# A new order for the instructions of an attention and gated-MLP kernel

## The chip, the cores and the metric

The kernel runs on one core of a Trainium2 chip. The metric is the device time of one execution in microseconds (us), the median of several runs. A profile, taken in an execution of its own, gives the start and length of every instruction on the engines: TensorE (PE, its weight loads PEld), VectorE (DVE), ScalarE (ACT), GpSimd (POOL) and the DMA queue of SyncE (SP).

## The reference

For 8 batches and 12 heads of 448 rows by 64, q and k are normalised row by row and scaled by g_q and g_k; softmax attention gives x of 448 by 768 for each batch. Then a gated MLP follows:

```
rmsnorm(x, g) = x / sqrt(mean(x*x) + 1e-6) * g
attn = softmax(rmsnorm(q) @ rmsnorm(k).T / sqrt(64)) @ v        # heads side by side: x [8, 448, 768]
h = relu(x @ w_in);  u, v = h[..., :512], h[..., 512:]
v_n = (v - mean(v)) / sqrt(var(v) + 1e-6)                       # over the 512
v_s = w_spatial @ v_n + b_spatial                               # over the 448 rows
out = (u * v_s) @ w_out                                         # [8, 448, 768], float32
```

## The kernel before

Four heads of one batch make a group; there are 24 groups, G = 0 to 23, three for each batch b. All instructions stand in one hand-scheduled program. A table of words, PLAN, is read from front to back; each word calls one small function that issues one step, and so the table alone sets the order in which each engine gets its instructions and the DMA queue its loads. A word reads name.arguments/slots/engine; the engine is a (ACT), v (DVE) or g (POOL). With i = 0 for q, 1 for k and 2 for v, the words of the attention are:

- L.G.i loads a group's q, k or v into one of ten raw tiles; l, q, r, i, j, n, p, k are the same steps in halves for group 0.
- Q squares a raw tile into sqt, R sums the squares on DVE, I and J (ACT) make 1/rms from the sums of q and k, N multiplies raw by it into nrm (bf16).
- P transposes nrm on PE and K copies it out of PSUM into qT or kT; later groups use T, a transposing DMA, and Z, which scales k.
- S.G.u makes two blocks of scores on PE (8 matmuls of 32 columns wide weights), E.G.u is their exp on ACT into et (168 of each).
- F.G casts v into vt. The words s, a and b sum et against ones and against the two halves of vt, for groups G and G+1 at once; D and d (ACT) make 1/sum; X (DVE) multiplies it in and gives x, transposed, in xt.

The words of the MLP: V (v half) and U (u half) multiply by w_in, W does the last 64 rows of V with the last 64 of the output of the batch before, c and u are the relu evictions, B, M, m, A the normalisation, H the spatial product, G the gate, O the product with w_out, o its eviction, t the store. wi.h.l loads an eighth of w_in from POOL's queue, ws, wo and wb the other weights; wx and y put w_spatial and b_spatial in place. The first V word of a batch needs X of one group of that batch and all of w_in; the third needs all three groups.

z.n and h.n are idle words on PE: n matmuls of the identity, 448 and 64 columns wide, whose results nobody reads.

PSUM has eight banks, and a word's slot digits name the banks or buffers that it takes; it waits until the last reader of what stood there is done. Between POOL and DVE there is one more rule, in port(): the squares, N, F and some others wait for the latest instruction of that kind that the table put on the other of the two engines, so these two take turns in the table's order.

## Time and profile before

| | |
|---|---|
| median of 3 runs | 268.88 us (268.8 to 270.5) |
| the profiled execution, its own time | 271.01 us |
| its span, first to last instruction | 268.9 us |
| mean granted TensorE clock | 0.998 |
| PE busy | 250.4 us (93%) |
| ACT busy | 220.6 us (82%) |
| DVE busy | 210.6 us (78%) |
| POOL busy | 127.8 us (48%) |
| moved by DMA | 55.48 MB, 206 GB/s over the span |

The span is what the profile's times add up to; the execution's own time has 2.1 us more around it. Busy shares are means over the whole span, so the table says only which engine is fullest, not what is waited for in any one stage. A row of the timeline has start, length, engine, line, operation, output and inputs, how many instructions are merged in it, and in brackets how long the engine was idle before and for whom.

### The profile page before, as it was taken

Reading aid. Unit: us, or ns where it says so; the run is one execution under the profiler, and the core shown is the slowest. Engines: PE = TensorE matmul, PEld = TensorE weight load, DVE = VectorE, ACT = ScalarE, POOL = GpSimd, SP = SyncE. Lnnn points to the kernel's source line nnn. Section 1 sums busy time; section 2 is a strip of 40 time slices with the busy share of each in tenths; the row PEclk is TensorE's granted clock in tenths of the full one; section 3 lists DMA queues with packets and bytes.
Section 4 is the critical chain, followed back from the end, with each engine's and each line's share of the span. In section 5 each row is a group of like instructions: output and inputs, shape, how many; then the busy total and the mean of one; then the engine's idle time right before and its main releaser. Section 6 shows DMA issues by size and latency. Waiting matters only on the chain.

```text
span 268.9 us, 10005 instructions
## 1 busy us (share of the span) xinstructions
PE 250.4 (93%) x4311; PEld 127.8 (48%) x4311; DVE 210.6 (78%) x363; ACT 220.6 (82%) x363; POOL 127.8 (48%) x99
## 2 busy tenths in 40 slices
PE   5997775999999997999999999999999999999993
...
GB/s 250 369 257 335 236 255 140 313 227 307 195 218 269 268 249 305 289 247 256 213 261 207 162 252 272 307 221 151 125 166 126 63 58 148 71 51 0 88 115 210
DMA packets 58462, 55.48 MB, mean 206 GB/s; under 512 B 34609, under 2 KB 54130, under 8 KB 58418
## 3 DMA queue, kind: packets, MB, share of 16 engines
...
q8 instruction: 33, 0.54, 0.8%
...
HBM read 38.55 MB, written 11.01 MB: 184 GB/s over the span
## 4 chain that ended last, share of the span: by engine, by line
PE 79%; DMA 9%; issue 4%; POOL 3%; ACT 2%; DVE 1%; POOLq 0%; DVEq 0%
PE ps L544 17%; PE ps L655 14%; PE ps L683 12%; PE ps L509 11%; PE ps L589 11%; PE ps L669 9%; DMA raw<-in_k_dram 8%; PE ps L618 4%; DMA raw<-in_q_dram 1%; POOL sqt L385 1%; POOL nrm L437 1%; ACT et L517 1%; ACT sqt L383 1%; POOL nrm L429 1%; DVE ss L396 0%
## 5 line engine op out<-in xcount | busy, mean ns | idle before, releaser
L517 ACT ACTIVATE et<-ps 128x896 bf16<-128x896 f32 x168 | 146.4, 926 | 12.7 <-PE ps L509 10.7
L429 POOL TENSOR_TENSOR nrm<-raw,rs 128x896 bf16<-128x896 f32 x37 | 62.0, 1688 | 41.9 <-ACT rs L414 34.3
L509 PE MATMUL ps<-qT,kT 64*32 64x448 bf16 x1344 | 56.0, 353 | 4.1 <-ACT et L517 2.3
L396 DVE TENSOR_REDUCE ss<-sqt 128x14 f32<-128x896 f32 x46 | 48.5, 1074 | 2.2 <-POOL sqt L385 2.2
L385 POOL TENSOR_TENSOR sqt<-raw 128x896 f32<-128x896 f32 x24 | 40.1, 1677 | 11.7 <-DVE nrm L429 4.3
L544 PE MATMUL ps<-et,vt 64*32 64x448 bf16 x1344 | 41.9, 349 | 3.6 <-issue 2.3
L655 PE MATMUL ps<-xt,w_in 128*128 128x448 bf16 x192 | 43.2, 353 | 0.0
L573 DVE TENSOR_TENSOR xt<-ps,rc 128x448 bf16<-128x448 f32 x48 | 27.9, 619 | 14.6 <-PE ps L544 8.8
L589 PE MATMUL ps<-w_in,xt 128*128 128x512 bf16 x144 | 37.8, 380 | 0.0
L683 PE MATMUL ps<-w_out,gt 128*128 128x384 bf16 x192 | 36.2, 327 | 0.4 <-ACT et L517 0.4
L509 PEld LDWEIGHTS <-kT 64*32 64x32 bf16 x1344 | 20.1, 90 | 28.2 <-issue 19.5
L544 PEld LDWEIGHTS <-vt 64*32 64x32 bf16 x1344 | 21.9, 92 | 15.1 <-issue 5.8
L669 PE MATMUL ps<-w_spT,vn 128*128 128x448 bf16 (+1 forms) x128 | 27.3, 353 | 0.0
L655 PEld LDWEIGHTS <-w_in 128*128 128x128 bf16 x192 | 17.6, 98 | 20.1 <-issue 4.8
L366 DVE COPY os<-ps 128x384 f32<-128x384 f32 (+1 forms) x32 | 17.6, 555 | 12.0 <-PE ps L683 7.9
L683 PEld LDWEIGHTS <-gt 128*128 128x128 bf16 x192 | 17.7, 98 | 16.5 <-issue 4.3
L674 DVE TENSOR_TENSOR gt<-ps,us 128x448 bf16<-128x448 f32 x32 | 19.0, 620 | 7.6 <-PE ps L669 5.5
L544 PE MATMUL ps<-et,ones 64*32 64x448 bf16 x672 | 23.5, 350 | 0.6 <-ACT et L517 0.6
L320 POOL CAST vt<-raw 128x896 bf16<-128x896 f32 x16 | 14.8, 930 | 18.1 <-DVE us L582 7.9
L630 DVE BATCH_NORM_STATS2 s<-vs 128x6 f32<-128x512 bf16 (+1 forms) x32 | 21.8, 680 | 1.4 <-ACT vs L580 0.9
L589 PEld LDWEIGHTS <-xt 128*128 128x128 bf16 x144 | 12.7, 98 | 17.0 <-issue 5.4
L364 ACT ACTIVATE os<-ps 128x384 f32<-128x384 f32 (+1 forms) x32 | 15.6, 490 | 6.2 <-PE ps L683 5.1
...
## 6 DMA issues: line engine op xcount, KB each, us to landing
...
```

The source lines that it names most:

```text
L385: port(eng, eng.tensor_tensor(out=t, in0=x, in1=x, op=ALU.mult))
L396: dve.tensor_reduce(out=sss[G % 3][:, i].rearrange("p r c -> p (r c)"), in_=sqt[where.pop(("sq", G, i))].rearrange("p r (c d) -> p (r c) d ...
L429: port(eng, eng.tensor_tensor(out=nrm[sl[0]].rearrange("p c r d -> p r c d"), in0=raw[where["raw", G, i]].rearrange("p r (c d) -> p r c d" ...
L509: pe.matmul(out=ps[at:at + 32, sl[n], 0:S], lhsT=kT[64 * r:64 * r + 64, c, 64 * hh + 32 * x:64 * hh + 32 * x + 32], rhs=qT[64 * r:64 * r + ...
L517: act.activation(out=ets[sl[0]].rearrange("q r (p c) -> q r p c", c=C), in_=ps[:, a:b + 1:b - a, 0:S].rearrange("q r (c p) -> q r p c", c= ...
L544: pe.matmul(out=ps[32 * l:32 * l + 32, where[kind, G][0], 0:S], lhsT=w, rhs=et_of(G, r, c)[at:at + 64], start=(n == 1), stop=(n == C), til ...
L573: dve.tensor_tensor(out=xts[b % 2][:, 2 * g + half, :], in0=ps[:, where.pop(("ab"[half], G))[0], 0:S], in1=rcs[where["rc", G]], op=ALU.mult)
L589: pe.matmul(out=ps[:, bank, :], lhsT=xts[b % 2][:, j, 128 * m:128 * m + 128], rhs=w_in[:, j % 2, j // 2, DH:], start=(n == 1 and j == 2 * ...
L630: dve.bn_stats(out=s6, in_=vss[b % SLOTS["vs"]][rows, m, :])
L655: pe.matmul(out=ps[:, bank, 0:S], lhsT=w_in[:, j % 2, j // 2, 128 * f:128 * f + 128], rhs=xts[b % 2][:, j, :], start=(n == 1 and j == 2 * ...
L669: pe.matmul(out=ps[:, sl[0], 0:S], lhsT=vns[b % SLOTS["vn"]][rows, m, 128 * f:128 * f + 128], rhs=w_spT[rows, m, :], start=(m == 0), stop= ...
L683: pe.matmul(out=ps[:, sl[0], 0:384], lhsT=gts[b % 2][:, f, 128 * m:128 * m + 128], rhs=w_out[:, f, 384 * h:384 * h + 384], start=(f == 0), ...
```

## The change

The table PLAN is replaced by another one of 1624 words, as many as before. The functions are the same. The number of words of each kind is the same but for the idle words: the first is z.13 with an h.5 behind it, where it was z.15, and the later ones are four with nine matmuls in all, where they were five with twelve. 76 words run on other engines. Net, on ACT there are one cast of v and one relu of V more and one full square, one half square, one Z, three output evictions, one relu of U and one y fewer; POOL has two casts and four squares more, one half square more, and five N fewer; DVE has five N, one Z, three output evictions, one relu of U and one y more, and three casts, three squares and one relu of V fewer. Slots, and with them banks and buffers, differ throughout, and most words stand a few places earlier or later.

```diff
-l.0.0/0/a l.1.0/1 gl.0//g l.0.1//a l.1.1 L.1.1/2 gl.1//g setup L.1.0/3 L.2.1/4 L.2.0/5 z.15/0 L.3.1/6 q.0.0/0/v
-L.3.0/7 q.1.0/1/a r.0.0 wb/0 r.1.0 L.4.0/8 q.0.1//a L.5.0/9 q.1.1//a r.0.1 i.0//a r.1.1 j.0//a n.0.0//g i.1//a j.1//a
...
+l.0.0/0/a l.1.0/1 gl.0//g l.1.1 l.0.1//a wb/0 gl.1//g setup L.1.1/2 L.1.0/3 L.2.1/4 z.13/0 h.5 L.2.0/5 q.0.0/0/v
+q.1.0/1/a L.3.0/6 r.0.0 L.4.0/7 r.1.0 L.3.1/8 q.1.1//g q.0.1//a L.5.0/9 i.0//a r.0.1 j.0//a n.0.0//g r.1.1 gA i.1//a
...
```

Three places follow, each as it stood and as it stands now.

The loads on SP's queue, from the first that needs a slot that was used before. rawN is the raw tile; the first six rows of before are the loads L.4.1, L.0.2, L.5.1, L.7.1, L.6.0 and L.3.2 (in two halves), then L.9.1, L.2.2 and L.6.1.

```order
L292 DMA raw1_65<-in_k_dram 128x2x448
L292 DMA raw2_66<-in_v_dram 128x2x448
L292 DMA raw3_67<-in_k_dram 128x2x448
L292 DMA raw4_68<-in_k_dram 128x2x448
L292 DMA raw5_69<-in_q_dram 128x2x448
L297 DMA raw7_71<-in_v_dram 64x2x448 x2
L292 DMA raw0_64<-in_k_dram 128x2x448
L292 DMA raw6_70<-in_v_dram 128x2x448
L292 DMA raw2_66<-in_k_dram 128x2x448
```

```order
L292 DMA raw1_65<-in_k_dram 128x2x448
L292 DMA raw2_66<-in_k_dram 128x2x448
L292 DMA raw3_67<-in_q_dram 128x2x448
L292 DMA raw4_68<-in_v_dram 128x2x448
L292 DMA raw5_69<-in_k_dram 128x2x448
L292 DMA raw0_64<-in_v_dram 128x2x448
L297 DMA raw6_70<-in_v_dram 64x2x448 x2
L292 DMA raw8_72<-in_k_dram 128x2x448
```

Now the order is L.4.1, L.5.1, L.6.0, L.0.2, L.6.1, L.2.2, L.3.2, L.7.1. The k of group 6 went from the ninth of these places, in raw2 behind v of group 0, to the fifth, in raw5 behind q of group 2.

POOL's list in the middle of the first three groups. The first row of both is N.3.1 (nrm1 of k, group 3).

```order
L429 TENSOR_TENSOR nrm1_78<-raw6_70,rs0_121 128x2x7x64
L320 CAST vt0_129<-raw2_66 128x896
L326 DMA w_in_153<-in_moe_w_in_dram 32x3x1024 x2
L385 TENSOR_TENSOR sqt2_76<-raw5_69 128x896
L326 DMA w_in_153<-in_moe_w_in_dram 32x3x1024 x4
L385 TENSOR_TENSOR sqt0_74<-raw2_66 128x896
L429 TENSOR_TENSOR nrm1_78<-raw9_73,rs2_123 128x2x7x64
```

```order
L429 TENSOR_TENSOR nrm1_78<-raw8_72,rs0_121 128x2x7x64
L385 TENSOR_TENSOR sqt0_74<-raw2_66 128x896
L320 CAST vt0_129<-raw4_68 128x896
L385 TENSOR_TENSOR sqt1_75<-raw3_67 128x896
L326 DMA w_in_153<-in_moe_w_in_dram 32x3x1024 x2
L429 TENSOR_TENSOR nrm3_80<-raw1_65,rs1_122 128x2x7x64
L326 DMA w_in_153<-in_moe_w_in_dram 32x3x1024
L429 TENSOR_TENSOR nrm0_77<-raw2_66,rs2_123 128x2x7x64
L326 DMA w_in_153<-in_moe_w_in_dram 32x3x1024
L385 TENSOR_TENSOR sqt0_74<-raw5_69 128x896
L429 TENSOR_TENSOR nrm1_78<-raw9_73,rs2_123 128x2x7x64
```

Between N.3.1 and N.5.0 (the last row) stood F.0, Q.6.0, Q.6.1 and six loads of w_in; now Q.5.1, N.4.1 and N.5.1 stand there too, and four loads of w_in. The square of k of group 6 (Q.6.1, the row before the last) stays next to N.5.0.

DVE's list at the same place, to the last X of group 2. xt0 is x of batch 0.

```order
L429 TENSOR_TENSOR nrm2_79<-raw8_72,rs1_122 128x2x7x64
L320 CAST vt1_130<-raw7_71 128x896
L429 TENSOR_TENSOR nrm3_80<-raw1_65,rs1_122 128x2x7x64
L573 TENSOR_TENSOR xt0_131<-ps_63,rc0_113 128x448
L396 TENSOR_REDUCE ss2_117<-sqt1_75 128x14
L366 COPY qT0_81<-ps_63 128x896
L320 CAST vt0_129<-raw6_70 128x896
L429 TENSOR_TENSOR nrm0_77<-raw3_67,rs2_123 128x2x7x64
L467 TENSOR_SCALAR kT0_87<-ps_63,g2_col_162 128x896
L573 TENSOR_TENSOR xt0_131<-ps_63,rc1_114 128x448 x2
L396 TENSOR_REDUCE ss0_115<-sqt0_74 128x14
L573 TENSOR_TENSOR xt0_131<-ps_63,rc0_113 128x448
```

```order
L429 TENSOR_TENSOR nrm2_79<-raw7_71,rs1_122 128x2x7x64
L573 TENSOR_TENSOR xt0_131<-ps_63,rc0_113 128x448
L320 CAST vt1_130<-raw6_70 128x896
L366 COPY w_spT_155<-ps_63 64x448
L366 COPY qT0_81<-ps_63 128x896
L385 TENSOR_TENSOR sqt2_76<-raw8_72 128x896
L467 TENSOR_SCALAR kT0_87<-ps_63,g2_col_162 128x896
L573 TENSOR_TENSOR xt0_131<-ps_63,rc1_114 128x448
L573 TENSOR_TENSOR xt0_131<-ps_63,rc0_113 128x448
L573 TENSOR_TENSOR xt0_131<-ps_63,rc1_114 128x448
L396 TENSOR_REDUCE ss0_115<-sqt0_74 128x14
L467 TENSOR_SCALAR kT1_88<-ps_63,g2_col_162 128x896
```

Before, the list was N.4.0, F.3, N.4.1, X.1.1, R.5.1, K.4.0, F.2, N.5.1, K.4.1, X.0.1 and X.0.0, R.6.1, X.1.0. Now it is N.4.0, X.1.1, F.3, y.3, K.4.0, Q.7.1, K.4.1, X.0.1, X.1.0, X.0.0, R.6.1, K.5.1: N.4.1 and N.5.1 are gone to POOL, F.2 to ACT, Q.7.1 has come, and X.1.0 stands ahead of R.6.1.

246 lines of the change are left out of this document (123 added, 123 removed).

## The prediction

> **What bounds the kernel now.** I read the busy times first, then the stretches, then the chain of waits and the timeline where the stretches leave holes.
>
> ```profile
> PE 250.4 (93%) x4311; PEld 127.8 (48%) x4311; DVE 210.6 (78%) x363; ACT 220.6 (82%) x363; POOL 127.8 (48%) x99
> core 0: us, PE busy (x) PEld busy (x) DVE busy (x) ACT busy (x) POOL busy (x), PEclk, DMA share, GB/s
> 0.00:10.00 10.00, 6.84 (x36) 3.38 (x37) 6.99 (x18) 6.12 (x11) 5.03 (x12) 1.00 0.85 297
> 10.00:20.00 10.00, 9.11 (x132) 4.18 (x130) 9.11 (x12) 9.89 (x16) 7.06 (x7) 1.00 1.12 289
> 20.00:30.00 10.00, 7.47 (x185) 4.03 (x184) 9.32 (x12) 9.78 (x16) 7.79 (x6) 1.00 0.94 288
> 30.00:40.00 10.00, 7.81 (x259) 5.10 (x258) 9.20 (x14) 9.71 (x17) 5.82 (x8) 1.00 1.01 265
> 40.00:50.00 10.00, 6.66 (x182) 3.29 (x179) 6.92 (x10) 7.12 (x13) 9.33 (x6) 1.00 1.05 186
> 50.00:60.00 10.00, 9.96 (x114) 4.33 (x107) 9.22 (x16) 9.97 (x16) 10.00 (x8) 1.00 1.28 277
> 60.00:70.00 10.00, 10.00 (x240) 5.05 (x238) 9.73 (x17) 9.82 (x20) 7.20 (x6) 1.00 1.04 269
> 100.00:110.00 10.00, 8.40 (x197) 4.38 (x182) 6.64 (x10) 8.25 (x16) 2.04 (x2) 1.00 1.10 328
> 260.00:270.00 10.00, 4.60 (x32) 2.45 (x30) 1.66 (x3) 2.91 (x6) 0.00 (x0) 0.88 0.46 178
> ```
>
> PE is idle for 18.5 us of 268.9. Of these 3.2 lie before 10 us, 8.9 between 10 and 50, 1.6 between 100 and 110, and 4.3 behind its last matmul; almost nothing is left for the rest. So there are two stages. Until about 48 us PE has only attention work, and ACT (9.89, 9.78, 9.71 of 10) and then a chain through POOL and DVE set the pace. From the first V word on, PE holds a stock of gated-MLP matmuls and is full. What the order can still win is an earlier first V word, and the few holes behind it. This is how the first stage ends:
>
> ```profile
> 30.82 0.37 SPq L292 DMA_DIRECT2D raw<-in_k_dram  x1
> 40.11 1.67 POOL L385 TENSOR_TENSOR sqt<-raw 128x896 f32<-128x896 f32 x1 [2.34 <-DMA raw<-in_k_dram]
> 41.82 1.09 DVE L396 TENSOR_REDUCE ss<-sqt 128x14 f32<-128x896 f32 x1 [2.22 <-POOL sqt L385]
> 42.82 0.62 DVE L573 TENSOR_TENSOR xt<-ps,rc 128x448 bf16<-128x448 f32 x1
> 43.49 0.38 PE L544 MATMUL ps<-et,vt 64*32 64x448 bf16 x8 [1.32 <-DVE xt L573]
> 47.90 1.47 PE L589 MATMUL ps<-w_in,xt 128*128 128x512 bf16 x6
> ```
>
> The load of k for G=6 (L.6.1) is issued at 30.82 and its square starts when it has landed, at 40.11; R.6.1 on DVE waits 2.22 us for that square, X.1.0 stands behind R.6.1, and PE waits 1.32 us for X.1.0's bank. The first V word starts at 47.90.
>
> Three of PE's holes have another cause:
>
> ```profile
> q8 instruction: 33, 0.54, 0.8%
> 41.58 0.27 PE L448 MATMUL ps<-ident,nrm 128*128 128x128 bf16 x2 [1.32 <-issue]
> 47.23 0.36 PE L544 MATMUL ps<-et,vt 64*32 64x448 bf16 x2 [0.70 <-issue]
> 104.47 0.37 PE L544 MATMUL ps<-et,vt 64*32 64x448 bf16 x4 [1.60 <-issue]
> ```
>
> Each falls inside a word, where no data is waited for. Counted over the words, the first two stand at matmuls 607 and 735, 128 matmuls or 256 PE instructions apart; the third is near 1756, eight such steps on. 0.54 MB in 33 packets are 16 KB each, so PE's own instructions arrive in blocks of 256, and three of 33 blocks came late: 3.6 us in all.
>
> **The change part by part.** Work that keeps its instructions and its engine costs nothing by being reordered while PE stays full. PE's matmuls number 4311 in both. From the first V word on, PE changes between 32-column tiles (S, a, b, s) and wider ones 96 times before and 98 times now; a change that cost as much as a whole narrow word, 0.19 (19 words in 3.60 us, below), would make 0.4, one that is free 0, and I take 0.2. Then the sum has three more terms: the first V word, the holes behind it, the tail.
>
> *Idle words.* Two of the first fifteen go, five of 64 columns come, three later ones go.
>
> ```profile
> 3.16 5.47 PE L252 MATMUL ps<-ident 128*128 128x448 bf16 x15 [3.16 <-POOL ident masks.py:199]
> ```
>
> One of the first costs 5.47/15 = 0.36 us. A 64-column word stands nowhere in the trace; between a seventh of that and the whole of it, five cost 0.3 to 1.8 us against 0.7 saved. I take 0: the exps set the pace there (ACT 9.89 of 10), and the later words lie in PE's idle time (9.11 and 7.47 of 10). Uncovered, the three are worth 1.1 us.
>
> *The first V word.* L.6.1 was the twentieth load tile and is the sixteenth, behind q6 and v0 and ahead of v2 and v3. It goes when N.2.0 frees its slot (the second of two in the first row below, 19.4), lands 9.3 us later as before, near 29, and is out of the way. What is late next is POOL itself: Q.5.1, N.4.1 and N.5.1 came to it from DVE (and Q.7.1 to DVE from ACT), and port() makes POOL and DVE wait for each other in the table's order. The w_in issues between, 0.59 each, fall into POOL's waits for DVE.
>
> ```profile
> 17.26 2.09 DVE L429 TENSOR_TENSOR nrm<-raw,rs 128x896 bf16<-128x896 f32 x2
> 26.98 1.69 POOL L429 TENSOR_TENSOR nrm<-raw,rs 128x896 bf16<-128x896 f32 x1 [0.74 <-DVE vt L320]
> L429 POOL TENSOR_TENSOR nrm<-raw,rs 128x896 bf16<-128x896 f32 x37 | 62.0, 1688 | 41.9 <-ACT rs L414 34.3 <-DVE vn L646 2.8 <-DVE nrm L429 1.8
> L385 POOL TENSOR_TENSOR sqt<-raw 128x896 f32<-128x896 f32 x24 | 40.1, 1677 | 11.7 <-DVE nrm L429 4.3 <-DVE kT L467 3.0 <-DMA raw<-in_k_dram 2.6
> L320 POOL CAST vt<-raw 128x896 bf16<-128x896 f32 x16 | 14.8, 930 | 18.1 <-DVE us L582 7.9 <-DVE kT L467 3.6 <-DVE vn L646 2.5
> L326 POOL DMA_DIRECT2D w_in<-in_moe_w_in_dram x8 | 4.7, 593 | 0.0
> DMA to landing us min/median/max: 6.6/8.1/9.7
> L429 DVE TENSOR_TENSOR nrm<-raw,rs 128x896 bf16<-128x896 f32 x9 | 9.7, 1087 | 1.2 <-POOL sqt L385 0.7 <-ACT rs L414 0.3
> L385 DVE TENSOR_TENSOR sqt<-raw 128x896 f32<-128x896 f32 x9 | 9.7, 1082 | 0.0
> L467 DVE TENSOR_SCALAR kT<-ps,g_col 128x896 bf16<-128x896 bf16 x7 | 4.7, 676 | 0.0
> L396 DVE TENSOR_REDUCE ss<-sqt 128x14 f32<-128x896 f32 x46 | 48.5, 1074 | 2.2 <-POOL sqt L385 2.2
> L573 DVE TENSOR_TENSOR xt<-ps,rc 128x448 bf16<-128x448 f32 x48 | 27.9, 619 | 14.6 <-PE ps L544 8.8 <-ACT rc L567 4.2 <-PE ps L509 1.4
> L320 DVE CAST vt<-raw 128x896 bf16<-128x896 f32 x8 | 5.3, 665 | 0.7 <-POOL nrm L429 0.5 <-POOL sqt L385 0.3
> 227.07 3.60 PE ps L544 x152
> ```
>
> Up to N.3.1, which ended at 28.67, POOL's new row has Q.4.1 later and w_spT's cast earlier; I take the same end. From there: Q.5.1 1.68, F.0 0.93, Q.6.0 1.68 give 32.96. DVE's N.4.0 must follow Q.6.0, and N.4.1 must follow it: 1.09 and 1.69, 35.74. Then DVE's F.3 0.66, POOL's N.5.1 1.69: 38.09. Now the last w_in load is issued (wi.0.1) and takes 6.6 to 9.7 us to land (the last row of that tile's view), 8.1 in the middle: 44.7 to 47.8, middle 46.2. DVE goes on: Q.7.1 1.08, K.4.1 0.68, three X 1.86, R.6.1 1.07, K.5.1 0.68: 43.5. K.5.1 frees the bank of a.2.5.1; behind that PE has ten words of 8 matmuls at 0.19 (the last row: 152 in 3.60), 45.4, and one block boundary, 0.70 if it is late again: 46.1. Both ends meet near 46.3, against 47.90: -1.6 us. Bounds: 45.4 with neither late load nor late block (-2.5), 48.5 with the slowest landing and a late block (+0.6).
>
> ACT is no narrower there: Q.7.1 and y.3 leave it and F.2 comes. A copy of that size on ACT is not in the trace; the square of as many elements is, so I take its 0.95, and POOL's 0.93 and DVE's 0.67 for the same copy lie below.
>
> ```profile
> L383 ACT ACTIVATE sqt<-raw 128x896 f32<-128x896 f32 x13 | 12.2, 953 | 0.0
> ```
>
> Q.7.1 and F.2 cancel, and were F.2 twice as long, the 2.9 us that ACT idles between 40 and 50 (7.12 busy) would hide it.
>
> *Behind it.* Leads from load and transpose to use stay mostly as they were, by the count of exps between; four v loads (G=6, 9, 10, 21) have two or three exps where five was the least, but POOL, which casts them, is idle for half of the span. I take 0, from -1.6 (the hole at 104.47 not met) to +1.6 (one more such).
>
> *Tail.* H.7.0 and H.7.2 now follow the other two at once, and two u evictions stand on DVE ahead of the last three G.
>
> ```profile
> 256.95 1.68 PE L669 MATMUL ps<-w_spT,vn 128*128 128x448 bf16 x8
> 257.58 1.71 DVE L674 TENSOR_TENSOR gt<-ps,us 128x448 bf16<-128x448 f32 x3 [0.68 <-ACT us L580]
> 258.47 5.36 PE L683 MATMUL ps<-w_out,gt 128*128 128x384 bf16 x32
> ```
>
> From the start of H.7.3: an H takes (258.47 - 256.95)/2 = 0.76, so the four end at 3.04 and two O words (5.36/8 = 0.67) at 4.38. DVE starts G.7.3 after the first H, about 0.95, and needs six operations at 0.57 to 0.62: 4.5 to 4.7. O.7.1.1 waits for the last: 0.1 to 0.3. I take +0.3.
>
> **Sum**, against the span of the profiled execution: 268.9 + 0.2 - 1.6 + 0.0 + 0.3 = **267.8**. That execution's own time was 271.01, 2.1 beyond its span; the median of the runs shown is 268.88, which is the span, so 267.8 stands for the median too.
>
> The Trainium skill, Runtime: NRT & Kernel Launch, Instruction fetch mechanics, says that an engine's next 16 KiB page is fetched while the current one runs and that crossing a boundary is mostly hidden. By it the three holes would be chance and need not come back. The trace agrees on the block size and shows three of 33 not hidden.
>
> **Rivals.** *No block is late* (chance 0.22): the order shifts which load burst each fetch meets. For it: thirty of 33 boundaries show nothing. Against: the first stage's DMA share stays near 1.0. Then the 1.60 at 104.47 goes, and with a quick w_in landing V starts at 45.4: 267.8 - 1.6 - 0.9 = 265.3.
>
> *POOL sets the first stage* (0.20, the slower side): POOL was idle 9.3 us of 10 to 40 (7.06, 7.79, 5.82 busy); now its list from Q.2.1 to wi.0.1 (7 squares, 4 nrm, a cast, 7 w_in issues, by the rows 23.6, and w_spT's cast, some 1.5) fills about 25 of the 27.7 us to 38.1, which leaves 2.6. Each further wait, for a v or k load or for rs from ACT, delays wi.0.1, N.5.1 and Q.6.1 one for one, and with them the first V word. From 1.1 us on nothing is won, from 3.8 the kernel is over 1% slower, and with all 9.3 it is 6.7. Midway between the last two, 5.2: 273.0. Against: its loads are issued earlier than they were.
>
> *The gain is given back* (0.20): after 48 us ACT is full as well (9.97, 9.82). If the exps come no earlier, PE meets them 1.6 us later: 269.4. Against: ACT has six fewer operations over the whole and idles 1.75 in 100 to 110.
>
> **How the numbers follow.** The forecast has 0.38, with its own range 266.5 to 269.6. The two rivals on either side are needed for 8 in 10: 265.0 to 273.0. One per cent, about what a measurement of this kernel can tell from no change, is 2.7 us: faster 0.22 (no late block), same 0.58 (forecast and given back), slower 0.20 (POOL).
>
> **What would show it.** Right: no DVE wait for Q.6.1's load, first L589 near 46.3 just after the last w_in landing, PE full behind it. Wrong: POOL idle over 4 us between 28 and 38, first L589 after 48.5, or new holes of over 2 us behind 50 us.

## The result, and the profile after

The changed kernel is slower: 276.33 us (median of 4, 276.19 to 276.7) against 269.69 for the kernel before in the same comparison, ratio 1.025 with an interval of 1.020 to 1.030. Run again later it gave 277.77 (median of 7) against 269.36, ratio 1.030 [1.025, 1.036]. The forecast was 267.8, with a range up to 273.0: the kernel was to become a little faster, and it became slower than the range allowed for.

The span of the profiled execution went from 268.9 to 274.4. Busy times and the instruction queue on the page of after:

```profile
PE 253.6 (92%) x4311; PEld 126.6 (46%) x4311; DVE 212.4 (77%) x367; ACT 218.8 (80%) x357; POOL 128.6 (47%) x101
...
q8 instruction: 33, 0.54, 0.9%
```

The stretches of after, in the columns shown of before:

```profile
10.00:20.00 10.00, 7.55 (x111) 3.22 (x109) 8.86 (x12) 9.82 (x16) 6.48 (x6) 1.00 1.11 303
20.00:30.00 10.00, 8.19 (x173) 3.72 (x170) 7.90 (x11) 9.86 (x15) 8.59 (x8) 0.83 1.08 303
30.00:40.00 10.00, 7.20 (x202) 4.54 (x203) 7.16 (x12) 8.11 (x15) 9.77 (x9) 0.95 1.08 256
40.00:50.00 10.00, 7.52 (x222) 4.51 (x222) 7.11 (x10) 7.53 (x11) 8.45 (x6) 0.88 1.06 179
90.00:100.00 10.00, 9.01 (x220) 4.74 (x219) 8.75 (x15) 8.36 (x14) 3.98 (x4) 1.00 0.98 239
100.00:110.00 10.00, 9.24 (x281) 4.22 (x260) 7.81 (x13) 8.85 (x13) 5.74 (x5) 1.00 0.99 264
120.00:130.00 10.00, 9.39 (x144) 4.05 (x142) 8.95 (x15) 9.29 (x16) 1.98 (x3) 1.00 1.07 289
```

POOL has become the fullest engine between 30 and 40 us (9.77 of 10, 5.82 before), ACT no longer is (8.11 against 9.71), and PE has holes between 90 and 110 and behind 120 us, where before only the stretch from 100 to 120 had any (1.60 and 0.45). PE's rows at these holes, from the timeline of after:

```profile
38.04 0.38 PE L448 MATMUL ps<-ident,nrm 128*128 128x128 bf16 x4 [1.03 <-issue]
44.78 0.36 PE L509 MATMUL ps<-qT,kT 64*32 64x448 bf16 x2 [0.29 <-issue]
50.16 0.55 PE L544 MATMUL ps<-et,vt 64*32 64x448 bf16 x10 [1.98 <-issue]
50.83 1.47 PE L589 MATMUL ps<-w_in,xt 128*128 128x512 bf16 x6
94.66 2.59 PE L669 MATMUL ps<-w_spT,vn 128*128 128x448 bf16 x12 [0.79 <-ACT et L517]
102.78 0.38 PE L544 MATMUL ps<-et,ones 64*32 64x448 bf16 x8 [0.73 <-DVE xt L573]
123.69 0.38 PE L509 MATMUL ps<-qT,kT 64*32 64x448 bf16 x8 [0.57 <-DVE kT L467]
212.40 0.38 PE L509 MATMUL ps<-qT,kT 64*32 64x448 bf16 x8 [0.83 <-DMA qT<-nrm]
```

The first V word starts at 50.83, not at 46.3. Three blocks of PE's instructions come late in the first stage, at matmuls 479, 607 and 735 (the waits for "issue"): 3.30 us in all, where before two of these were late (2.02). Behind 90 us PE waits at H.1.0, s.8.2.1, S.12.1 and S.23.1. The block near matmul 1756 is not late any more.

As PE has the same 4311 matmuls, the start of one and the same matmul number (counted from 0) can be set side by side. Where matmul records were missing in a later run (up to 16), the count was taken from the weight loads, which are complete. In us, after minus before:

| matmul | before | after | difference |
|---|---|---|---|
| 351 | 30.98 | 32.54 | +1.56 |
| 753 (first V word) | 47.90 | 50.83 | +2.93 |
| 1247 | 81.56 | 84.68 | +3.12 |
| 1503 | 94.73 | 99.67 | +4.94 |
| 1887 | 116.29 | 120.01 | +3.72 |
| 2143 | 129.63 | 134.60 | +4.96 |
| 3551 | 204.07 | 208.80 | +4.73 |
| 4280 (near the end) | 259.93 | 265.46 | +5.53 |

So 2.9 us came before the first V word, 2.0 between it and matmul 2143, 0.8 behind matmul 3551, where S.23.1 waits 0.83, and the tail (matmul 4191 to the end) is the same to 0.1.

### The profile page after: what moved, and what is told of

It is laid out like the page before. It is cut to its first block, busy times and chain, and to the rows that moved or that the text cites. A ratio compares the mean times of both kernels' runs of the same rounds, so it can differ in the third digit from the quotient of the medians.

```text
span 274.4 us, 10034 instructions
## 1 busy us (share of the span) xinstructions
PE 253.6 (92%) x4311; PEld 126.6 (46%) x4311; DVE 212.4 (77%) x367; ACT 218.8 (80%) x357; POOL 128.6 (47%) x101
## 4 chain that ended last, share of the span: by engine, by line
PE 52%; DMA 4%; DVE 2%; ACT 1%; POOL 1%; issue 1%; SPq 0%; DVEq 0%; POOLq 0%; ACTq 0%
PE ps L544 11%; PE ps L683 9%; PE ps L655 9%; PE ps L589 7%; PE ps L509 7%; PE ps L669 7%; PE ps L618 3%; DMA kr<-nrm 2%; DMA qT<-nrm 2%; ACT et L517 1%; POOL nrm L429 1%; SPq L297 0%; DVE os L366 0%; DVE ss L396 0%; DVE xt L573 0%
## 5 line engine op out<-in xcount | busy, mean ns | idle before, releaser
L517 ACT ACTIVATE et<-ps 128x896 bf16<-128x896 f32 x168 | 144.8, 922 | 14.9 <-PE ps L509 13.9
L429 POOL TENSOR_TENSOR nrm<-raw,rs 128x896 bf16<-128x896 f32 x32 | 53.6, 1686 | 30.8 <-DVE nrm L429 9.5
L509 PE MATMUL ps<-qT,kT 64*32 64x448 bf16 x1344 | 57.8, 358 | 3.6 <-DVE kT L467 1.1
L385 POOL TENSOR_TENSOR sqt<-raw 128x896 f32<-128x896 f32 (+1 forms) x29 | 47.8, 1652 | 9.1 <-DMA raw<-in_k_dram 3.5
L544 PE MATMUL ps<-et,vt 64*32 64x448 bf16 x1344 | 42.5, 352 | 3.2 <-issue 2.0
L655 PE MATMUL ps<-xt,w_in 128*128 128x448 bf16 x192 | 42.2, 353 | 0.0
L589 PE MATMUL ps<-w_in,xt 128*128 128x512 bf16 x144 | 37.1, 380 | 0.0
L320 POOL CAST vt<-raw 128x896 bf16<-128x896 f32 x18 | 16.7, 929 | 39.8 <-DMA raw<-in_v_dram 12.4
L366 DVE COPY os<-ps 128x384 f32<-128x384 f32 (+1 forms) x35 | 19.2, 554 | 14.0 <-PE ps L618 6.6
L544 PEld LDWEIGHTS <-vt 64*32 64x32 bf16 x1344 | 20.7, 93 | 14.9 <-issue 4.2
L544 PE MATMUL ps<-et,ones 64*32 64x448 bf16 x672 | 25.3, 374 | 0.8 <-DVE xt L573 0.7
L364 ACT ACTIVATE os<-ps 128x384 f32<-128x384 f32 (+1 forms) x29 | 14.1, 489 | 12.1 <-PE ps L683 10.6
L589 PEld LDWEIGHTS <-xt 128*128 128x128 bf16 x144 | 12.6, 97 | 17.6 <-issue 6.1
```

Source lines behind the costliest of these rows:

```text
L385: port(eng, eng.tensor_tensor(out=t, in0=x, in1=x, op=ALU.mult))
L429: port(eng, eng.tensor_tensor(out=nrm[sl[0]].rearrange("p c r d -> p r c d"), in0=raw[where["raw", G, i]].rearrange("p r (c d) -> p r c d" ...
L509: pe.matmul(out=ps[at:at + 32, sl[n], 0:S], lhsT=kT[64 * r:64 * r + 64, c, 64 * hh + 32 * x:64 * hh + 32 * x + 32], rhs=qT[64 * r:64 * r + ...
L517: act.activation(out=ets[sl[0]].rearrange("q r (p c) -> q r p c", c=C), in_=ps[:, a:b + 1:b - a, 0:S].rearrange("q r (c p) -> q r p c", c= ...
L544: pe.matmul(out=ps[32 * l:32 * l + 32, where[kind, G][0], 0:S], lhsT=w, rhs=et_of(G, r, c)[at:at + 64], start=(n == 1), stop=(n == C), til ...
L589: pe.matmul(out=ps[:, bank, :], lhsT=xts[b % 2][:, j, 128 * m:128 * m + 128], rhs=w_in[:, j % 2, j // 2, DH:], start=(n == 1 and j == 2 * ...
```

## The experiments

Executions of one and the same kernel differ here by several us (the kernel before: 267.7 to 275.8 us), so most verdicts rest on one place in a trace, read by matmul number; a ratio stands where it carries one.

**A block or data?** The first idle words are cut otherwise, so that every later block begins 36 matmuls earlier in the program.

```diff
-z.13/0 h.5
+z.1/0 h.53
```

> The changed kernel with the first idle words cut otherwise: z.1 and h.53 where z.13 and h.5 stood, about as long (5.4 us for 5.5) but 36 matmuls more, so that every later block of 256 PE instructions begins 36 matmuls earlier in the program. Theory of the instruction blocks: the gaps that no data explains move to the new boundaries, a.0.2.1, s.2.3.1 and a.2.6.1, and P.4.0, S.4.4 and a.2.4.1 show none any more; from the boundary at matmul 479 to the one at 735 still pass 12 us or a little more. Rival, these gaps are waits for data that the records miss: they stay at P.4.0, S.4.4 and a.2.4.1. The time: by the first theory anything from 274.5 to 277.5, as the first V word now stands 54 matmuls behind a boundary and not 18; by the rival 276.3.

It took 278.29 us (ratio 1.027). The gaps moved: P.4.0, S.4.4 and the old a.2.4.1 show none, and the two left stand at a.2.6.1 (matmul 735) and a.4.6.1 (1119), exactly on new boundaries. Rows of the timeline of this run:

```profile
50.62 0.38 PE L542 MATMUL ps<-et,vt 64*32 64x448 bf16 x8 [0.76 <-issue]
73.12 0.38 PE L542 MATMUL ps<-et,vt 64*32 64x448 bf16 x6 [2.43 <-issue]
```

The rival, waits for data, falls. The time, above the 274.5 to 277.5 that the theory gave, had another cause, told under the hardware below: PE was slower at the start, and matmul 351 of the old count came 4.2 us later than in the changed kernel.

**Do the blocks stand behind the loads?** Nine raw loads (eight in the order before) move one of 128 rows and leave out the others; old rows stand in the tiles instead. Each thinned kernel (c1, c2, d1, d2, d3) ran once.

```diff
+        if (G, i) in THIN:
+            one = bass.AP(tensor=rows.tensor, offset=rows.offset, ap=[[C * D, 1], [2 * S * D, 2], [1, C * D]])
+            engines["s"].dma_start(out=raw[sl[0]][0:1], in_=one)
+            return
```

> The changed kernel with nine raw loads cut to one of their 128 rows (k and q of groups 7 and 9, k and q of group 8, v of groups 4 and 5, q of group 10): the tiles hold old rows instead, and the same instructions run on the engines. About 3.4 MB fewer are moved between 28 and 56 us; no PE instruction is changed. Theory that PE's instruction blocks are late because they stand behind the loads: the block's packet starts within 1.5 us of the crossing, the gaps at matmuls 479, 607 and 735 are under 0.3 each, and the first V word starts at 48.3 or earlier. Rival, block fetches are slow by themselves or a dependence is what PE waits for: gaps of over 1 us stay at one of these three.

> The kernel before with eight raw loads cut to one of their 128 rows in the same stretch (k and q of group 9, q of group 7, k and q of group 8, v of groups 4 and 5, q of group 10). Theory of the loads: no gap at matmuls 607 and 735 (1.32 and 0.70 before), the load of k for group 6 lands earlier as well, and the first V word starts at 44.5 to 46.0 instead of 47.9. Rival: the gaps at 607 and 735 stay, first V word at 47 or later.

PE's waits for issue in the changed kernel with thinned loads, from the view of waits between 28 and 52 us (in total, times, longest), and the row of its first V word from the timeline:

```profile
PE ps L595 <- issue: 0.2, 1, 0.2
```

```profile
47.08 0.39 PE L595 MATMUL ps<-w_in,xt 128*128 128x512 bf16 x1
```

The first V word of the order before with thinned loads:

```profile
44.88 0.39 PE L595 MATMUL ps<-w_in,xt 128*128 128x512 bf16 x1
```

No block at 479, 607 or 735 was late in either, nor in the three thinned variants further down (d1, d2, d3). Of the fifteen profiles with full loads all but one (a5) have at least one late there. The first V word came 3.75 us earlier in the changed order and 3.0 in the old one (where k of group 6 also landed earlier): PE's instructions were late while the queues were full of loads. But the changed order is still 2.2 later than the old, so the late blocks are not what sets the two apart.

**Are the blocks late by the order or by the execution?** The changed kernel once more, as it is.

> The changed kernel again as it is, to see whether late instruction blocks belong to the order or to the execution. The third experiment had the same instructions in the same order up to 100 us, and its blocks at matmuls 479, 607 and 735 cost 0.6 us in all, against 4.2 in the first profile of the changed kernel. Theory of the order (the blocks are late in nearly every execution): spans within 0.7 us of 274.4, in this profile 3 to 5 us lost at the three boundaries. Rival, each execution draws them anew: spans spread over 271 to 278, as the four of the third experiment did (272.1 to 277.4).

Spans of 274.3 to 276.7 in six executions, and 280.7 in the profiled one, which lost 5.8 at the three boundaries. Neither theory holds as put: the spans are steadier than by the rival and less steady than by the first. (The 0.6 and 4.2 us that the expectation names are 0.2 and 3.3 by the waits for issue alone.) The variants a1, a3, a4, a5 and ab have the changed order up to the first V word (a1 and a4 with one bank altered) and give further draws, ba and b1 of the old one. The profiles of a0, a6 and b4, which were among their kernels' longest executions and lost 5.8, 6.4 and 5.7 us at these blocks, are left out:

| kernel, head | waits for issue at 479, 607, 735 | first V word |
|---|---|---|
| after, changed | 3.3 | 50.83 |
| a1, changed | 4.4 | 51.34 |
| a3, changed | 0.2 | 48.45 |
| a4, changed | 1.3 | 47.85 |
| a5, changed | 0 | 47.88 |
| ab, changed | 3.4 | 51.41 |
| before | 2.0 | 47.90 |
| b1, L.6.1 early | 2.0 | 46.76 |
| ba, before | 1.9 | 46.23 |

The same words lost 0 to 4.4 us. The mean is 2.1 for the changed head and 2.0 for the old one. The first V word without these waits is at 46.6 to 48.3 with the changed head (mean 47.5) and at 44.3 to 45.9 with the old (mean 45.0): about 2.5 us that belong to the order, by a plain subtraction.

**The part that the gain rested on, alone.** In the kernel before, L.6.1 and L.9.1 change places.

```diff
-L.9.1/0 L.2.2/6 wi.0.3 L.6.1/2
+L.6.1/0 L.2.2/6 wi.0.3 L.9.1/2
```

> The kernel before with one part of the change alone: L.6.1 and L.9.1 change places on SP's queue (and their raw tiles with them), so that k of group 6 is issued near 28 us and not at 30.8. It takes away the wait that the prediction took as the bound of the first stage: Q.6.1's wait for the load, R.6.1's for the square, X.1.0's. Prediction's theory (this chain sets the first V word): X.1.0 comes 1.3 to 2.2 us earlier, the first V word at 46.0 to 46.6 instead of 47.9, the time 1.3 to 1.9 below the kernel before. Rival, the instruction blocks set it: the block that starts at a.2.2.1 is late by as much more, the first V word stays at 47.4 to 48.2 and the time within 0.5 of the kernel before.

The timeline of this run, R.6.1 and X.1.0 on DVE, then PE at the late block and the first V word:

```profile
39.87 1.08 DVE L394 TENSOR_REDUCE ss<-sqt 128x14 f32<-128x896 f32 x1
40.87 0.62 DVE L571 TENSOR_TENSOR xt<-ps,rc 128x448 bf16<-128x448 f32 x1
46.08 0.36 PE L542 MATMUL ps<-et,vt 64*32 64x448 bf16 x2 [1.40 <-issue]
46.76 1.47 PE L587 MATMUL ps<-w_in,xt 128*128 128x512 bf16 x5
```

R.6.1 waits for nothing and starts 1.95 us earlier than before, X.1.0 too; a block eats part of it (1.40 for 0.70), and the first V word is 1.15 earlier (46.0 to 46.6 was expected), the end of the trace 1.7. The time is 269.84 (10 runs) against 271.36, ratio 0.995 [0.991, 0.999]. The prediction's term is right in kind for this part by itself, and this kernel is the only one with full loads here that beats the kernel before, by half a per cent.

**Head or rest?** Two crosses of the tables, cut just behind the first V words, where the tile slots and banks of both orders agree: *ab* is the changed head (all that stands ahead of the cut) with the old rest, *ba* the old head with the changed rest.

> A cross of the two orders: the changed table up to c.0.0, just behind the first V words (its first 286 words), and from there the words not yet used in the order of the table before, with that table's slots and engines (the states fit without a relabelling). Theory of two separate losses: the first stage of the change is worth +2.9 at the first V word, and behind it the old order loses nothing to itself, so the cross ends 2 to 3 us above the kernel before, about 271.5 of span against 268.9, and 3 us below the changed kernel. Rival, all comes from the first stage (its loads and POOL's list leave later groups late): as slow as the changed kernel, 274 to 276 of span. Rival on the other side, all comes from behind: as fast as the kernel before.

> The cross the other way: the table before up to c.0.0 (its first 284 words), and from there the remaining words in the order, slots and engines of the changed table. Theory of two separate losses: the first V word at 47.9 as before, and then the holes of the changed order between 90 and 130 us and at 212: 2.6 us more than the kernel before, if they only add up; 4 to 5 more if that order gives an earlier start back, as the changed kernel with fewer loads did (0.8 us ahead at the first V word, 4.0 behind at matmul 2143). So 271.5 to 274 of span. Rival, all comes from the first stage: as fast as the kernel before, 268 to 269.5.

ab: 274.65, ratio 1.014 [1.008, 1.021]. In its trace the first V word is 3.5 later than before (51.41, with 3.4 in late blocks), and from there on nothing is added: +3.50 at matmul 2143, +3.70 at the end. ba: 276.33, ratio 1.023 [1.018, 1.027], with a first V word at 46.23, 1.7 earlier than before, +4.65 at 2143 and +5.40 at the end. So the rest of the changed order alone costs nearly what the whole change costs: 1.4 and 2.3% apart, 2.5 to 3.0% together. By the intervals the two losses could still just add up; the traces show that they do not, as ba starts its V words 4.6 us ahead of the changed kernel and is level with it at matmul 1247 (84.82 and 84.68). An early start is given back. A stretch of both shows where (ab, then ba; PE's columns alone), and then the rows of ba:

```profile
70.00:80.00 10.00, 10.00 (x104) 1.00 1.12 192
70.00:80.00 10.00, 7.53 (x77) 0.93 0.85 186
```

```profile
68.69 0.92 POOL L318 CAST vt<-raw 128x896 bf16<-128x896 f32 x1 [8.90 <-DMA raw<-in_v_dram]
69.59 4.98 POOL L427 TENSOR_TENSOR nrm<-raw,rs 128x896 bf16<-128x896 f32 x3
74.53 1.67 POOL L383 TENSOR_TENSOR sqt<-raw 128x896 f32<-128x896 f32 x1
76.24 1.09 DVE L427 TENSOR_TENSOR nrm<-raw,rs 128x896 bf16<-128x896 f32 x1 [4.10 <-POOL sqt L383]
77.24 0.62 DVE L672 TENSOR_TENSOR gt<-ps,us 128x448 bf16<-128x448 f32 x1
77.91 0.32 PE L681 MATMUL ps<-w_out,gt 128*128 128x384 bf16 x1 [1.96 <-DVE gt L672]
```

F.6 on POOL waits 8.90 us for the v load of group 6, and three N and the square Q.12.1 stand behind it. The square ends at 76.20; DVE's N.9.1, whose turn comes behind it, starts at 76.24 after 4.10 us of waiting; the gate behind N.9.1 in DVE's list comes 1 us later, and O.0.0.1 on PE waits 1.96. In the changed kernel itself F.6 waits for another engine, N.9.1 only 0.36 us for its turn, and PE, which arrives at O.0.0.1 4 us later, does not wait there.

**Separate holes in a full PE?** First the two transposing DMAs that PE met too early, then four repairs at once, then two.

```diff
-T.12.0/1 S.11.5/01 ... V.2.2.1 T.12.1/1
+T.12.0/1 T.12.1/1 S.11.5/01 ... V.2.2.1
-T.23.1/0 S.20.4/01 ... a.18.5.1/01 T.23.0/2
+T.23.1/0 T.23.0/2 S.20.4/01 ... a.18.5.1/01
```

> The changed kernel with two transposing DMAs issued earlier on SP's queue: T.23.0 directly behind T.23.1 and T.12.1 directly behind T.12.0, each as soon as its N is written. Theory: the PE gaps of 0.92 us at 123.7 (ahead of S.12.1) and 1.19 at 212.4 (ahead of S.23.1) go, and as PE is full around them both are kept: 276.3 - 1.6 = 274.7 (274.4 to 275.2). Rival, something else is late at the same places (the exps, or SP's queue is held by these transposes and a later load is late): the gaps move and the time stays within 0.5 of 276.3.

It took 275.55 us (ratio 1.015 [1.007, 1.023]), but not for the reason given. S.23.1's gap is gone. In the place of S.12.1's, O.1.2.1 waits for an eviction of u on DVE, and a new gap stands at S.15.2:

```profile
119.63 0.32 PE L681 MATMUL ps<-w_out,gt 128*128 128x384 bf16 x1 [0.73 <-DVE us L580]
142.82 0.38 PE L507 MATMUL ps<-qT,kT 64*32 64x448 bf16 x8 [0.98 <-DMA qT<-nrm]
```

From the first V word to matmul 4280 this run took 2.7 us more than the kernel before, the changed kernel 2.6: nothing was won behind 50 us. What made it faster is the first stage, with 0.2 instead of 3.3 at its late blocks. The rival is right about the gaps: they moved.

```diff
-p.1.1/0
+p.1.1/7
-Q.15.0/0/a A.1.1 ... E.9.5/0/a T.10.1/1 R.15.0 H.1.0/6
+A.1.1 ... E.9.5/0/a Q.15.0/0/a T.10.1/1 H.1.0/6
-O.1.0.0/2 E.9.4/j/a X.6.1 S.9.3/34 X.7.1 s.8.2.1/56 S.8.6/01
+E.9.4/j/a X.6.1 S.9.3/34 X.7.1 s.8.2.1/26 S.8.6/01 O.1.0.0/5
-a.18.5.1/01 T.23.0/2
+a.18.5.1/01
```

T.23.0 goes behind T.23.1 as above, R.15.0 ahead of R.15.1, and from s.8.2.1 on banks 2 and 5 are exchanged in all words.

> The changed kernel with four small repairs: p.1.1 in the free bank 7; T.23.0 directly behind T.23.1 (T.12.1 stays); Q.15.0 on ACT behind E.9.5 instead of ahead of E.8.4 (R.15.0 with it), so that H.1.0's bank comes free earlier; s.8.2.1 in banks 2 and 6, with O.1.0.0 behind S.8.6 in bank 5. Theory that the holes behind 90 us are separate waits that add up: from matmul 1247 to the last, 2.5 to 3.0 us less than in the changed kernel (H.1.0 0.9, s.8.2.1 0.8, S.23.1 0.95). Rival, ACT is as full as PE there and each repaired wait comes back a few words later: under 1.2 us less. The first stage is left as it is, so the whole time depends on its blocks as well: 272.5 to 276.0.

It took 305.02 us, far slower, and is a test of its theory only up to about matmul 1503. There H.1.0's gap is gone (+0.84 against before at 1503, +4.94 in the changed kernel, with first V words at -0.05 and +2.93). Behind it the exchange of two bank numbers put 47 of the 168 S words into banks that are not neighbours (1 and 5, 2 and 4, 2 and 6, 3 and 5), and 30 us were lost in small waits from there to the end. That the banks are the cause was not tried by itself and is not shown.

```diff
-Q.15.0/0/a A.1.1 ... E.9.5/0/a T.10.1/1 R.15.0 H.1.0/6
+A.1.1 ... E.9.5/0/a Q.15.0/0/a T.10.1/1 H.1.0/6
-T.23.1/0 S.20.4/01 ... a.18.5.1/01 T.23.0/2
+T.23.1/0 T.23.0/2 S.20.4/01 ... a.18.5.1/01
```

> The changed kernel with two repairs behind 90 us and nothing else: T.23.0 directly behind T.23.1, and on ACT Q.15.0 behind E.9.5 instead of ahead of E.8.4 (R.15.0 goes with it), so that H.1.0's bank comes free about 0.95 us earlier. Theory that these holes are separate waits in a full PE: from matmul 1247 to the last 1.6 to 2.0 us less than the changed kernel needed (0.9 at H.1.0, 0.95 at S.23.1), which is 178.8 from 84.68 to 263.5 at the run's end of the table. Rival, ACT's and DVE's work only moves and the next words wait instead (s.8.2.1, O.1.2.1, S.12.1): under 0.8 less.

It took 277.13 us, ratio 1.030. From matmul 1247 to 4280 it took 181.6 us against 180.8 in the changed kernel: nothing was won. (R.15.0 moves as in a4.) Both repaired gaps are gone, and the next word that could wait did. Rows of POOL, DVE and PE in this run:

```profile
95.19 0.93 POOL L318 CAST vt<-raw 128x896 bf16<-128x896 f32 x1 [4.49 <-DMA raw<-in_v_dram]
97.72 1.69 POOL L427 TENSOR_TENSOR nrm<-raw,rs 128x896 bf16<-128x896 f32 x1
99.44 0.45 DVE L465 TENSOR_SCALAR kT<-kr,g_col 128x896 bf16<-128x896 bf16 x1 [3.08 <-POOL nrm L427]
101.01 0.38 PE L542 MATMUL ps<-et,ones 64*32 64x448 bf16 x8 [3.02 <-DVE xt L571]
```

F.9 on POOL waits 4.49 us for the v load of group 9 (L.9.2); Q.15.1 and N.12.0 stand behind it; N.12.0 ends at 99.41, Z.10 on DVE, whose turn comes after it, starts at 99.44; X.6.0 and X.6.1 stand behind Z.10, and s.8.2.1 needs the bank of X.6.1. The same chain, shorter, is in the profile after (F.9, N.12.0, then Z.10 and the X):

```profile
96.95 0.93 POOL L320 CAST vt<-raw 128x896 bf16<-128x896 f32 x1 [2.76 <-DMA raw<-in_v_dram]
99.48 1.69 POOL L429 TENSOR_TENSOR nrm<-raw,rs 128x896 bf16<-128x896 f32 x1
101.21 0.45 DVE L467 TENSOR_SCALAR kT<-kr,g_col 128x896 bf16<-128x896 bf16 x1 [0.79 <-POOL nrm L429]
```

In the table before, F.9 is on DVE and behind all four X, and so is Z.10.

**The chain, taken away and put in.** a6 is a5 with Z.10 behind X.7.1 (first edit); b4 is the kernel before with T.10.1 later and Z.10 ahead of X.6.0 (second).

```diff
-X.7.0 ... Z.10/2/v ... X.6.0 ... X.6.1 ... X.7.1
+X.7.0 ... X.6.0 ... X.6.1 ... X.7.1 Z.10/2/v
```

```diff
-E.8.0/a/a T.10.1/1 ... u.1.0//v H.1.0/7 ... X.7.0 ... X.6.0 ... X.7.1 ... S.9.0/67 Z.10/2/v
+E.8.0/a/a ... u.1.0//v T.10.1/1 H.1.0/7 ... X.7.0 Z.10/2/v ... X.6.0 ... X.7.1 ... S.9.0/67
```

> The fifth variant (T.23.0 and Q.15.0 repaired) with one more word moved: Z.10, the scaling of k of group 10 on DVE, which waits for its transposing DMA, goes from ahead of X.6.0 to behind X.7.1, where the order before has it. There PE waited 3.4 us at s.8.2.1 for the bank that X.6.1 frees, after DVE had idled 3.1. Theory of Z.10: the gap at s.8.2.1 falls to under 0.6, and of the 2.9 us that were lost between matmuls 1503 and 1631 at least 2 stay won at matmul 1887. Rival, the transposing DMA of group 10 is itself late and S.10.5, some 60 matmuls on, waits for it as long: a new gap of over 1.5 at the first S of group 10 and no gain at 1887.

> The kernel before with one part of the change alone: T.10.1 issued just ahead of H.1.0 and Z.10 placed behind X.7.0, ahead of X.6.0, as in the changed table. Theory of Z.10: DVE idles for the transposing DMA, PE gets a gap of 1 to 3 us at s.8.2.1, at matmul 1631 the kernel is 1 to 3 us later than before, and part of it stays to the end (1 to 2 us, as ACT and PE are both full behind). Rival: the DMA lands in time when the rest of the order is the old one, gap under 0.5 and no change.

a6: its four executions spread from 273.3 to 282.5, so only the place counts. The gap at s.8.2.1 is gone. Z.10 now waits for POOL behind the X, the two evictions of o behind Z.10 are late, and b.8.3.1 waits for their bank:

```profile
104.50 0.45 DVE L465 TENSOR_SCALAR kT<-kr,g_col 128x896 bf16<-128x896 bf16 x1 [1.98 <-POOL nrm L427]
107.92 0.38 PE L542 MATMUL ps<-et,vt 64*32 64x448 bf16 x8 [2.34 <-DVE os L364]
```

From matmul 1503 to 1887 a6 lost 0.9 against before, a5 1.7: less than half of the 2 us expected. The wait is moved, not removed. Both theories had its agent wrong: not the transposing DMA but POOL's N releases Z.10, which starts within 0.05 us of its end in after, a5, a6 and b4.

b4: 272.23 (10 runs), ratio 1.005 [1.0005, 1.009]. Its rows (N on POOL, Z.10, then PE at the s word):

```profile
97.82 3.34 POOL L427 TENSOR_TENSOR nrm<-raw,rs 128x896 bf16<-128x896 f32 x2 [2.73 <-DMA kr<-nrm]
101.19 0.46 DVE L465 TENSOR_SCALAR kT<-kr,g_col 128x896 bf16<-128x896 bf16 x1 [2.03 <-POOL nrm L427]
102.77 0.57 PE L542 MATMUL ps<-et,ones 64*32 64x448 bf16 x16 [2.35 <-DVE xt L571]
```

Two words are moved, and PE has a hole of 2.35 in an order that had none there; at matmul 1887 2.1 us of it are left, and about 1.3 us, by the ratio, in the time. What starts this chain is another thing than in a5: N.12.0 waits 2.73 us for the moved transposing DMA, since it writes the tile nrm3 that T.10.1 still reads. So b4 shows that the turns pass a wait on down to PE; that a v load starts it is told from the rows of after, a5 and ba alone.

**What makes the head later?**

```diff
 a1
-p.1.1/0
+p.1.1/7
 a7, d1
-Q.7.1/2/v a.0.4.1 ... K.4.1/0/v ... X.0.1 ... X.0.0
+a.0.4.1 ... K.4.1/0/v ... X.0.1 ... X.0.0 Q.7.1/2/v
 d2
-N.4.1/3/g
+N.4.1/3/v
```

a1 gives p.1.1 a free bank; bh has the first 55 words of the order before and then the changed one; a7 puts Q.7.1 behind X.0.0. a7 lost 3.3 us at late blocks and settles nothing, so d1, d2 and d3 ask without late blocks, each one edit against c1: Q.7.1 behind X.0.0; N.4.1 on DVE; the first 55 words of the order before.

> The changed kernel with one slot altered: p.1.1 writes to bank 7, which nobody has used, and no longer to bank 0, where k.0.0 on ACT still reads p.0.0. Theory of the bank: the gap of 1.35 us ahead of p.1.1 at 11.2 us goes, S.0.0 starts about 0.9 us earlier. Then two ways: if the 0.9 is carried to the end, 276.3 becomes 275.4; if blocks of PE's instructions set the pace at 38 to 50 us, the late blocks grow by as much, the first V word stays within 0.4 us of 50.8 and the time within 0.4 of the changed kernel's. Rival, the bank conflict is not the cause of the late start and PE waits there for k.0.0 or kT anyway: S.0.0 moves by under 0.3.

> The changed kernel with the start of the order before: its first 55 words (to J.1, with q.1.1 on ACT, the loads in the order before, z.15 for z.13 and h.5), then the remaining words as in the changed table. Theory that the start carries the lateness: matmul 95 at 15.0 to 15.2 instead of 15.5 to 16.1, N.3.1 on POOL ends 0.6 to 1.2 earlier than 29.97, matmul 351 at 31.0 to 31.4. Rival, it arises later, between S.0.0 and N.3.1 (order of squares and loads): matmul 351 stays over 31.8. The whole time should hardly follow (275 to 277 of own time), since what the head wins is given back between 77 and 130 us.

> The changed kernel with Q.7.1 on DVE behind X.0.0 and no longer ahead of K.4.1. In the profile without late blocks DVE idled 1.07 there for its turn behind POOL's N.5.1, and PE then waited 0.9 us at S.3.2 for the bank that X.0.1 frees. Theory that POOL's list sets the first stage through these turns: K.4.1 and the X come 1.5 to 2.1 us earlier, the gap at S.3.2 goes, matmul 620 comes 0.8 to 1.2 earlier than 43.5 where no block is late. Rival: the exps set it (ACT is full to 40 us); S.3.2 or the word behind it waits for ACT instead, and matmul 600 stays near 42.9.

> The changed kernel with the nine loads thinned as before (one row of 128 is moved, old rows stand in the tiles), and Q.7.1 on DVE behind X.0.0 instead of ahead of K.4.1. Against the thinned kernel without the edit, where DVE idled 1.07 us for its turn and PE waited 0.60 at S.3.2 (at 42.03). Theory of POOL's list through the turns: K.4.1 starts at 38.8 to 39.2 instead of 40.8, no wait at S.3.2, matmul 620 at 42.0 to 42.6 instead of 43.47, first V word at 45.6 to 46.6 instead of 47.08. Rival, the exps: matmul 620 stays above 43.2.

> The changed kernel with the nine loads thinned, and N.4.1 back on DVE, as in the order before: POOL's list between N.3.1 and Q.6.1 is 1.69 us shorter, DVE's 1.09 longer. Theory that POOL's list sets the first stage: P.4.1 and N.5.1 come 0.6 to 1.7 us earlier, and the first V word at 46.0 to 46.7 instead of 47.08. Rival, N.5.1 waits for its nrm tile (PE's P.4.0) and DVE has more to do: within 0.3 of 47.08, or later.

> The changed kernel with the nine loads thinned and the first 55 words of the order before. Its sister with full loads had matmul 351 at 31.75 and the first V word at 47.08, with 1.08 lost at one late block. Theory that the start is worth what it saves at matmul 351 and no more: 351 at 31.4 to 31.8 (31.87 without), first V word 0.1 to 0.6 earlier, 46.5 to 47.0. Rival, the start works on through loads and blocks: 46.3 or earlier.

The times are medians, those of the thinned kernels single executions, and the starts are from the one profile of each (a0's is its longest execution). In bh and d3, which have three idle matmuls fewer, the count is shifted by three.

| kernel | time | matmul 95 | 351 | 490 | first V word | from 490 to it |
|---|---|---|---|---|---|---|
| before | 268.88 | 14.98 | 30.98 | 35.49 | 47.90 | 12.4 |
| a0 | 277.77 | 15.55 | 32.07 | 38.40 | 53.33 | 14.9 |
| a1 | 277.2 | 15.68 | 32.10 | 38.21 | 51.34 | 13.1 |
| bh | 272.98 | 15.53 | 31.75 | 36.55 | 47.08 | 10.5 |
| a7 | 278.32 | 15.62 | 32.13 | 38.67 | 51.83 | 13.2 |
| c2, thinned, order before | 267.32 | 15.14 | 30.99 | 35.50 | 44.88 | 9.4 |
| c1, thinned | 274.26 | 15.51 | 31.87 | 37.89 | 47.08 | 9.2 |
| d1, thinned | 279.07 | 19.95 | 37.59 | 42.24 | 52.08 | 9.8 |
| d2, thinned | 273.05 | 15.56 | 31.91 | 36.70 | 46.23 | 9.5 |
| d3, thinned | 272.15 | 15.34 | 31.55 | 36.19 | 45.94 | 9.8 |

a1: S.0.0 starts at 11.85; with the old bank it started at 11.7 in a0 and 12.2 in the first profile. The bank is not the cause; the rival is right. Late blocks (4.4) and, from 51.5 to 54.9 with PE full, a stretch at half the clock (between matmuls 753 and 863 it took 1.6 us more than the profile after) made the time.

d2 and d1 speak against the theory that POOL's list sets the way from matmul 490 to the first V word. With N.4.1 on DVE (d2), or with Q.7.1 out of the X words' way (d1), it takes 9.5 and 9.8 us; d3, where both stand as in the changed table, takes 9.8, and c2, the old order, 9.4. In d1 the words before S.3.2 came sooner, and the next waited as much longer. d2's first V word at 46.23 is what that theory expected, and d3's at 45.94 what its rival expected; but both are read against c1, which lost about 1.2 us to a stretch at half the clock (32.1 to 35.5 us) that d2 and d3 have not. (d1 lost 5 us to the clock at its start.)

What is left is +0.9 at 351 and +1.2 at 490 (d2 against c2), most of it there by matmul 351. The rows tell where that comes from: of after, the square Q.4.1 on POOL, N.3.0 on DVE and matmul 351 on PE, then N.3.0 before.

```profile
23.93 1.38 POOL L326 DMA_DIRECT2D w_in<-in_moe_w_in_dram  x2
25.33 1.69 POOL L385 TENSOR_TENSOR sqt<-raw 128x896 f32<-128x896 f32 x1
27.05 1.09 DVE L429 TENSOR_TENSOR nrm<-raw,rs 128x896 bf16<-128x896 f32 x1 [1.81 <-POOL sqt L385]
32.54 0.38 PE L544 MATMUL ps<-et,vt 64*32 64x448 bf16 x8 [1.18 <-DVE w_spT L366]
```

```profile
24.73 1.09 DVE L429 TENSOR_TENSOR nrm<-raw,rs 128x896 bf16<-128x896 f32 x1 [0.68 <-POOL sqt L385]
```

Before, Q.4.1 followed Q.4.0 on POOL and ended at 24.70. In the changed table F.1 on DVE takes its turn between the two (24.01 to 24.64 in after), and two loads of w_in are issued on POOL there (to 25.31): Q.4.1 ends at 27.02, and N.3.0, which must follow it, starts 2.3 us later than before. From there DVE has no idle time to y.1, which ends at 32.55, as PE starts matmul 351 in the bank that it frees. The wait of N.3.0 is 1.81 or 1.82 in after, c1, d2, d3 and bh, and in d3, whose Q.4.0 ends 0.2 later than before, Q.4.1 ends 1.3 later. So here too the turns pass lateness on; no run takes this place out by itself. The old start takes back 0.3 to 0.4 at 351 in d3, as expected there; bh was expected at 31.0 to 31.4 and came at 31.75, 0.3 ahead of a0.

bh as a whole missed what was expected of it: 272.98, ratio 1.011 [1.007, 1.016], and not 275 to 277. The first 55 words are worth more than their 0.4 us, and bh loses 3.2 us from the first V word to matmul 2143, ba 6.3. Why the start reaches that far stays open.

## Why the prediction was wrong

Two terms of the sum failed, the first V word and what comes behind it.

**The first V word** was the term of -1.6; it measured +2.9, at 50.83 for 46.3. Its parts:

- L.6.1 earlier is worth what was said: R.6.1 does not wait, 1.95 us earlier in b1 alone, and no DVE wait for it in the profile after.
- "Up to N.3.1, which ended at 28.67 ... I take the same end" failed. The timeline of after has N.3.1 and, further on, N.5.1 on POOL and K.5.1 on DVE:

```profile
28.29 1.68 POOL L429 TENSOR_TENSOR nrm<-raw,rs 128x896 bf16<-128x896 f32 x1 [0.73 <-PE ps L509]
37.93 1.68 POOL L429 TENSOR_TENSOR nrm<-raw,rs 128x896 bf16<-128x896 f32 x1
43.83 0.67 DVE L467 TENSOR_SCALAR kT<-ps,g_col 128x896 bf16<-128x896 bf16 x1
```

N.3.1 ends at 29.97, 1.3 late, N.5.1 at 39.61 for 38.09 (+1.5), K.5.1 at 44.50 for 43.5 (+1.0). The reckoning from row to row held to half a microsecond; its origin was taken over from the old trace although the words ahead of it had all been moved. The prediction saw Q.4.1 go back in POOL's list and let the w_in issues "fall into POOL's waits for DVE"; ahead of Q.4.1 two of them and F.1's turn did not (the rows above), N.3.0 started 2.3 us late, and N.3.1 had to follow it.
- "One block boundary, 0.70 if it is late again" was a side term. The profile has three, 3.30, which is 2.6 of the 4.5 us between forecast and profile, and other executions of the same words 0 to 6.4. As the old head has 2.0 on average as well, this is not what the change costs; it is what a single profile of this kernel cannot tell from the order. The Trainium skill, Runtime: NRT & Kernel Launch, Instruction fetch mechanics, calls the crossing of a 16 KiB boundary mostly hidden. While loads fill the queues it often is not here (1.98 us at one boundary in the profile after, 2.43 in a2); with thinned loads it is (0.2 in all).

Of what the forecast gave as signs of itself being wrong, "first L589 after 48.5" came true, and so did "new holes of over 2 us behind 50" (2.9 us in four holes). The third did not: POOL was idle for 0.5 us between 28 and 38, not for over 4.

**Behind it, 0 from -1.6 to +1.6**, is the step that decided: with the changed rest, even the old head's early first V word won nothing (ba). It measured +2.6 from the first V word to matmul 4280 in the profile, 7.1 with the old head in front. The prediction saw that the v loads of groups 6, 9, 10 and 21 stand closer to their use, and set it aside because POOL "is idle for half of the span". That POOL has time does not matter: it waits for L.9.2 with N.12.0 behind it in its list, and DVE waits for its turn behind N.12.0 with Z.10 ahead of the X words; in ba the same goes from L.6.2 through F.6 and N.9.1. Leads were counted from load to use only, not through port() to what stands behind on the other engine. This chain is what the rows show for one of the four holes of the profile after, 0.73 us at s.8.2.1 (3.02 in a5). The other three end with an exp on ACT (0.79), a scaling of k on DVE (0.57) and a transposing DMA (0.83), and their causes were repaired (a3, a5) but not followed further.

**The rivals.** *POOL sets the first stage* was on the right side. POOL's list was full, as that rival reckoned (9.48 of 10 busy between 28 and 38), but the further waits that it needed did not come there (0.16 and 0.65 between 30 and 43), and taking words out of the way (d1, d2) won 0.3 us at most from matmul 490 on. What it had in kind, a wait passed on by the turns, shows in the rows ahead of N.3.1 and, from v loads, 50 us further on. *The gain is given back* is true in kind: in ba, c1 and a5, with first V words from 1.7 us ahead of the kernel before to level with it, PE is 3.5 to 4.7 us behind it at matmul 2143. It is no fixed pace (a3 is 1.6 behind, d3 0.6). It was priced as if PE would at worst keep the old pace. *No block is late* did not happen in the profile; where it did, in a5, the kernel was still slower than the one before (span 273.0 against 268.9).

**Idle words, 0**: no run changes them alone in the way of the forecast. A 64-column word takes 0.054 us (in a2), so the five cost 0.3, the lower bound that the prediction gave. **Tail, +0.3**: 0.0, matmul 4191 to the last. **Tile changes, 0.2**: no row shows it.
